# A top-32 attention kernel with routed experts: GpSimd compares the count and multiplies, VectorE only sums, when three thresholds are chosen

## The chip, the cores and the metric

One NeuronCore of a Trainium2 chip runs the whole program. The metric is the device time of one execution in microseconds (us). Engines go by their names in the profile: PE is TensorE, DVE is VectorE, ACT is ScalarE, POOL is GpSimd, SP is SyncE, which only starts DMAs here.

## The reference

Attention for 8 batches of 8 heads, 576 rows of 64 columns, in which each row of scores keeps only its 32 largest; then a layer of 8 experts that routes each of the 4608 tokens to one expert.

```python
scores = scale * np.matmul(q, k.transpose(0, 1, 3, 2))
kth = np.partition(scores, -top_k, axis=-1)[..., -top_k:-top_k + 1]
scores = np.where(scores >= kth, scores, -1000000000.0)
attn = softmax(scores); out = np.matmul(attn, v)
...
logits = x @ w_gate + modality_bias[modality_id]
e_idx = np.argmax(logits, axis=1)
out[mask] = gate_w[mask, None] * (np.maximum(x[mask] @ w1[e], 0.0) @ w2[e])   # for each e
```

## The kernel before, in words

The scores are worked on in 288 tiles of 128 rows by 576 columns; a pair of heads makes nine tiles. The loop `for i in range(LAST)` (line 887) takes one step for each tile, and a step holds one stage of each of the tiles in flight, so that tile i is multiplied while older tiles are further on. The order of the instructions on each engine is the order in which the loop issues them; no scheduler changes it.

What a tile goes through:

- `qk` and `sevac` (lines 323 and 340): the scores, and their copy to SBUF by ScalarE.
- `subs` and `chain` (lines 346 and 351), on VectorE: seven maxima over sevenths of the row (L349) give 56 candidates, and a chain of MAX8 and MATCH_REPLACE8 over these (L360 to L362) gives the 24 largest, `mg[.., 0:24]`.
- `below` (line 370, L374 on GpSimd) sets a bias just below the 24th value; `sign` (L381 on ScalarE) compares the row with it and counts, into `n`, how many values lie below; `pool_y` (L387 on GpSimd) multiplies the row by that comparison, and `find` (L391 on VectorE) takes the next eight values out of the product into `mg[.., 24:32]`.
- `pick` (line 393), once for three tiles: `eq` (L398) compares the count `n` with nine possible counts, `jk` (L399) multiplies the hits by the nine candidates `mg[.., 23:32]`, and a sum (L400) leaves the one threshold of each tile in `kth`. All three are VectorE's, on 128 x 27 numbers.
- `keep` (L411 on VectorE) is the mask: it compares the row with `kth` and multiplies the exponentials `ex` by the result. For two tiles in three of the first 48, `hide` (L418), `hidden` (L424 on GpSimd) and `masked` (L430) do this in another way.
- `trans`, `evac`, `av`: the transposes and the product with v.

Step i handles `chain` of tile i - 1, `pool_y` of tile i - 4, `find` of tile i - 5 and `keep` of tile i - 7 (LY, LT and LR, lines 39 to 41). When (i - 5) % 3 is 2, it also chooses the thresholds of tiles i - 7, i - 6 and i - 5, and the first of these is masked in the same step, right behind. Such a step is called a choosing step below; there are 96.

VectorE's order in a step (lines 1008 to 1047): the chain (`a_`) woven with the maxima and `find` (`b_`), then the list `c_`: `pick`, small work of the routing and of the experts, and `keep` last. Up to four of the seven maxima are held back and put between the last entries of `c_` (HOLD, lines 1040 to 1044), so that an instruction of `pick` does not stand directly behind the one whose result it reads.

GpSimd's order in a step: what `c_` holds for it (the scatter DMAs of finished tokens, `send`, line 562, L564 and the memset L490 behind it; a few copies), then `gate` (L434), `pool_y`, `below`, `small` (L368), `fill` (L314) and at the end the DMAs of expert results (L754). `gate` reads one number of the last tile's mask, so `pool_y` starts only when VectorE has finished the mask of the step before.

The experts' work is issued beside the attention as TensorE has room by a table of costs, and goes on behind it; from about 1060 us on only experts are left.

Of the kernel before, what the change touches and what calls it, by code (L numbers as in the profile page):

```python
# [14 lines left out]
OP = mybir.AluOpType  # L15
AX = mybir.AxisListType
# [22 lines left out]
LY = KL + 2  # L39
LT = LY + 1  # L40
LR = LT + 2
# [30 lines left out]
def kernel(  # L72
# [13 lines left out]
    V, A, G, PE, SP = nc.vector, nc.scalar, nc.gpsimd, nc.tensor, nc.sync  # L86
# [27 lines left out]
    LD, PR, T = {}, {}, {}  # L114
# [43 lines left out]
    def fiota(name, shape, pattern, base, cm):  # L158
        t = const.tile(shape, FT, name=name)
        G.iota(t, pattern=pattern, base=base, channel_multiplier=cm, allow_small_or_imprecise_dtypes=True)  # L160
        return t

    i9s = fiota("i9s", [128, 3, 9], [[0, 3], [2, 9]], S - 2 * TOPK, 0)
# [19 lines left out]
    kth = const.tile([128, NT], FT, name="kth")  # L183
# [200 lines left out]
    def pool_y(i):  # L384
        t = T[i]
        t["y"] = wk.tile([128, S], FT, name="y", bufs=YB)
        G.tensor_tensor(t["y"], t["S"], t["K"], op=OP.mult)  # L387

    def find(i):
        t = T[i]  # L390
        V.max(t["mg"][:, i % 3, 24:32], t["y"])  # L391

    def pick(i):

        t = T[i]
        eq, v = (wk.tile([128, 3, 9], FT, name=nm, bufs=1) for nm in ("eq", "jk"))
        n = t["n"][:, 0, :]
        return [lambda: V.tensor_tensor(eq, i9s, n[:, :, None].to_broadcast([128, 3, 9]), op=OP.is_equal),  # L398
                lambda: V.tensor_tensor(v, eq, t["mg"][:, :, 23:32], op=OP.mult),  # L399
                lambda: V.tensor_reduce(kth[:, i - 2:i + 1], v, axis=AX.X, op=OP.add)]  # L400

    def expo(i):
        t = T[i]
# [28 lines left out]
    def gate(i):  # L432

        G.tensor_scalar(spare[:, 0:1], T[i]["P"][0:1, 0:1], 1.0, 1.0, op0=OP.mult, op1=OP.mult)  # L434
# [247 lines left out]
    def expert(s, act, nxt, whole, defer):  # L682
# [82 lines left out]
        if nxt:  # L765
            pick, rows, done, tok = sched(s + 1, whole)
            todo = pick + done + rows + tok
            c, k = len(todo) - 2, 2 if whole else 3
            cut = [min(k * x, c) for x in range(CUT[0])] + [c + 1] * (CUT[1] - CUT[0]) + [c + 2]

            def both(f, a, b):
                f()
                chore.extend(todo[a:b])
                if not defer:
                    chores()
            n = len(cut) - 1
            return [(c, lambda f=f, a=a, b=b: both(f, a, b), w) for (c, f, w), a, b in zip(main, cut, cut[1:])] + main[n:]
# [13 lines left out]
    def ready(n, whole):  # L791
        pick, rows, done, tok = sched(n, whole)
        for f in pick + done + rows + tok:
            f()
        for g in range(4):
            load_w1(n, g)
        for g in range(4):
            load_w2(n, g)
# [4 lines left out]
    def more_moe():  # L803
# [14 lines left out]
        elif full >= n + 1:  # L818
            now = SL[n - 1] if moe else {"xt": True, "used": [4, 4]}
            if not now["xt"]:  # L820
                return
            plan.update(ready=n, go=False)
            pick, rows, done, tok = sched(n, fits(n))
            free = []

            def begin():
                free.extend(now["used"])
                now["nxt"] = True

            def take(x, g):  # L830
                return lambda: (load_w1, load_w2)[x](n, g) if g < free[x] else None
            l1 = [take(0, g) for g in range(4)]
            l2 = [f for g in range(4) for f in (take(1, g), PAUSE)]
            go = [lambda: plan.update(go=True)]
            if n == 0:
                def sent():

                    while sends:
                        sends.popleft()()
                rush.extend(pick + [begin] + l1[:2] + done + [PAUSE, sent] + rows + [PAUSE, l1[2], l1[3], PAUSE] + tok + go)  # L840
            else:
                rush.extend(pick + [begin] + rows + l1[:1] + done + [PAUSE, l1[1], PAUSE, l1[2], l1[3], PAUSE] + tok + go)
            side.extend(l2)

    def weave(a, b):

        nb, na, kb = len(b), len(a), 0
        for x in range(na):
            a[x]()
            e = (x + 1) * nb // na  # L850
            while kb < e:
                b[kb]()
                kb += 1
        while kb < nb:
            b[kb]()
            kb += 1
# [22 lines left out]
    ok = lambda x: 0 <= x < NT  # L879
    early = lambda u: u < EARLY and u % 3 != 2  # L880
# [6 lines left out]
    for i in range(LAST):  # L887
# [120 lines left out]
        a_, b_, c_ = [], [], []  # L1008
# [4 lines left out]
        if ok(i - LT):  # L1013
            b_.insert(2, lambda: find(i - LT))
            if (i - LT) % 3 == 2:
                c_ += pick(i - LT)
        for x, f in enumerate(lo):
            b_.insert(LOP[x] if x < len(LOP) else len(b_), f)
        small_ = []
# [20 lines left out]
        if ok(i) and len(c_) > 1:  # L1040
            n = min(len(c_) - 1, HOLD)
            held, b_ = b_[len(b_) - n:], b_[:len(b_) - n]
            m = len(c_) - n
            c_ = c_[:m] + [f for pair in zip(held, c_[m:]) for f in pair]
        weave(a_, b_)
        for f in c_:
            f()

        for f in moves:
            f()  # L1050

        if ok(i - 1 - LR) and not early(i - 1 - LR):
            gate(i - 1 - LR)
        if ok(i - LY):
            pool_y(i - LY)
        if ok(i - 1):
            below(i - 1)
        if ok(i - 2) and (i - 2) % 3 == 2:
# [264 lines left out]
```

## Time and profile before

| what | us |
|---|---|
| median of 3 runs | 1294.63 (1292.91 to 1297.9) |
| profiled execution | 1286.85 |
| its span, first to last instruction | 1285.1 |
| VectorE busy in the span | 1157.5 (90%) |
| TensorE busy (matmuls) | 1183.2 (92%) |
| ScalarE busy | 996.6 (78%) |
| GpSimd busy | 665.8 (52%) |

The profiled execution is 7.8 us below the median of the timed runs. Shares are averages over the attention (to about 1060 us) and the experts' tail. A duration in the profile runs from an instruction's start to its end; the next one of the same engine can start before that end, so what an instruction costs its engine is read from start to start.

### The profile page before, as it was taken

What the parts mean: (1) busy time and instruction counts of PE and PEld (TensorE: products, weight loads), DVE (VectorE), ACT (ScalarE), POOL (GpSimd) and SP (SyncE); (2) the same over time, 40 slices, a digit from 0 to 9 for tenths busy, and PEclk for the clock granted to TensorE, in tenths of its full rate; (3) what the DMA queues carried; (4) which work ended last, traced back from release to release, by engine and by line L of the source; (5) the groups of instructions that cost most, each with busy time, mean ns of one, the idle gap of its engine ahead of it and who ended that gap; (6) DMA issues with size and microseconds to landing.
All of it is one profiled execution on the core that took longest, in us unless ns stands there. A gap on an engine that the chain in (4) does not pass through costs nothing. (4 is left out here: it accounts for less than half of the span.)

```text
span 1285.1 us, 29038 instructions
## 1 busy us (share of the span) xinstructions
PE 1183.2 (92%) x8117; PEld 934.1 (73%) x8117; DVE 1157.5 (90%) x5948; ACT 996.6 (78%) x2029; POOL 665.8 (52%) x1249
## 2 busy tenths in 40 slices
PE   5789887999988999999999999999999999999996
PEld 4667676767766778686777868777777766789885
DVE  4999999999999999999999999999999992767752
ACT  3799988888888988888898889888988773446542
POOL 2688866555474557554755575556655562110110
PEclk8899999999999999999999999999999999999998
DMA  6565336765347745755665665656766433657550
GB/s 125 125 183 142 89 85 183 198 156 149 85 128 189 216 124 154 199 158 127 194 169 159 168 187 147 171 143 171 170 154 168 132 122 115 234 186 266 204 171 15
DMA packets 206755, 201.05 MB, mean 156 GB/s; under 512 B 106221, under 2 KB 153325, under 8 KB 206576
## 3 DMA queue, kind: packets, MB, share of 16 engines
q1 hardware_dynamic: 198896, 178.59, 52.6%
q0 software_dynamic: 6256, 19.69, 4.2%
q8 instruction: 69, 1.13, 0.4%
q10 hardware_dynamic: 1424, 0.74, 0.2%
q14 instruction: 110, 0.90, 0.2%
HBM read 118.63 MB, written 24.23 MB: 111 GB/s over the span
## 5 line engine op out<-in xcount | busy, mean ns | idle before, releaser
L349 DVE MAX8 cand<-Ssb 128x8 f32<-128x82 f32 (+1 forms) x2016 | 429.4, 230 | 17.9 <-ACT Ssb L342 17.7
L387 POOL TENSOR_TENSOR y<-Ssb,K 128x576 f32<-128x576 f32 x288 | 367.8, 1277 | 1.9 <-ACT K L381 1.6
L336 PE MATMUL S<-ks,qs 128*128 128x288 f32 x1024 | 230.1, 347 | 43.1 <-ACT Ssb L342 24.5
L342 ACT ACTIVATE Ssb<-S 128x576 f32<-128x576 f32 x288 | 188.7, 655 | 91.4 <-PE S L336 61.7
L381 ACT ACTIVATE K<-Ssb,n 128x576 bf16<-128x576 f32 x288 | 227.5, 790 | 25.3 <-POOL y L387 25.1
L336 PEld LDWEIGHTS S<-ks,qs 128*128 128x128 f32 x1024 | 157.4, 192 | 97.0 <-issue 40.5
L391 DVE MAX8 mg<-y 128x8 f32<-128x576 f32 x288 | 214.4, 745 | 2.7 <-POOL y L387 2.7
L405 ACT ACTIVATE ex<-Ssb,sm 128x576 f32<-128x576 f32 x256 | 200.3, 782 | 0.0
L453 ACT ACTIVATE PT<-T 128x640 f32<-128x640 f32 (+1 forms) x288 | 191.1, 663 | 9.5 <-PE T L445 9.5
L727 PE MATMUL E<-xgT,w1b 128*128 128x256 f32 x768 | 187.6, 387 | 6.8 <-ACT hT L731 3.1
L411 DVE SCALAR_TENSOR_TENSOR P<-Ssb,kth,ex 128x576 f32<-128x576 f32 x224 | 188.6, 842 | 0.3
L739 PE MATMUL E<-w2b,hT 128*128 128x512 f32 x384 | 179.6, 596 | 3.0 <-ACT ot L749 1.7
L445 PE MATMUL T<-idf,P 128*128 128x128 f32 x1152 | 171.9, 277 | 9.5 <-ACT P L430 8.9
L727 PEld LDWEIGHTS E<-xgT,w1b 128*128 128x128 f32 x768 | 139.8, 192 | 31.6 <-ACT hT L731 6.4
L434 POOL TENSOR_SCALAR spare<-P 1x1 f32<-1x1 f32 x224 | 43.6, 195 | 201.7 <-DVE mg L360 186.8
L445 PEld LDWEIGHTS T<-idf,P 128*128 128x128 f32 x1152 | 136.0, 141 | 16.7 <-ACT P L430 13.3
L473 PE MATMUL X<-PT,vm 128*64 128x256 f32 (+1 forms) x1536 | 145.6, 332 | 2.4 <-DVE cand L349 1.1
L374 POOL TENSOR_SCALAR n<-mg 128x1 f32<-128x1 f32 x288 | 72.8, 253 | 133.6 <-DVE mg L362 127.0
L473 PEld LDWEIGHTS X<-PT,vm 128*64 128x64 f32 x1536 | 89.2, 137 | 47.8 <-issue 10.1
L739 PEld LDWEIGHTS E<-w2b,hT 128*128 128x128 f32 x384 | 67.2, 190 | 60.6 <-issue 53.2
L1166 POOL DMA_INDIRECT out_dram<-ot,tk x14 | 14.0, 1003 | 132.3 <-ACT ot L1165 132.3
L862 PE MATMUL E<-idf,onesb 128*128 128x256 bf16 x436 | 63.1, 285 | 0.0
(212 smaller groups left out, 2295.8 us busy)
## 6 DMA issues: line engine op xcount, KB each, us to landing
w1b<-in_moe_w_dram SPq DMA_DIRECT2D x76, 512.0 KB, 5.0
w2b<-in_moe_w_dram SPq DMA_DIRECT2D x76, 512.0 KB, 4.9
qs<-st SPq DMA_DIRECT2D x126, 144.0 KB, 3.5
ks<-st SPq DMA_DIRECT2D x63, 288.0 KB, 3.8
ks<-st SPq DMA_DIRECT2D x62, 256.0 KB, 5.2
xg<-xs SPq DMA_DIRECT2D x19, 516.0 KB, 3.9
km<-in_k_dram SPq DMA_DIRECT2D x64, 128.0 KB, 3.5
vm<-in_v_dram SPq DMA_DIRECT2D x32, 256.0 KB, 3.2
```

What stands on the lines that cost most here:

```text
L336: PE.matmul(ps[:, hf, u - a:v - a], l, d["ks"][:, x, h, u + o:v + o], start=(n == 0), stop=(n == len(terms) - 1), skip_group_check=(j == 8))
L342: A.activation(sb.rearrange("p (a b) -> p a b", a=2), T[i]["ps"][:, :, :288], AF.Copy, scale=0.125)
L349: return [lambda s=s: V.max(c[:, s * 8:s * 8 + 8], T[i]["S"][:, bnd[s]:bnd[s + 1]]) for s in range(NSUB)]
L381: A.activation(t["K"], t["S"], AF.Sign, scale=2.0 ** -24 - 1.0, bias=t["n"][:, 1, i % 3:i % 3 + 1], accum_out=t["n"][:, 0, i % 3:i % 3 + 1])
L387: G.tensor_tensor(t["y"], t["S"], t["K"], op=OP.mult)
L391: V.max(t["mg"][:, i % 3, 24:32], t["y"])
L405: A.activation(t["ex"], t["S"], AF.Exp, bias=t["s"][:, i % 3:i % 3 + 1])
L445: PE.transpose(T[i]["pt"][:, x, :], (Pm if c == 4 else Pb[c % 2])[:, h * 512 + x * 128:h * 512 + x * 128 + 128], idf)
L453: A.activation(o, T[i]["pt"][:, :n], AF.Copy)
L473: PE.matmul(o.rearrange("p (a b) -> p a b", a=2) if j < 8 else o, l, r, start=(c == 0), stop=(c == 4))
L727: PE.matmul(ps[:, f % 2], w1b[:, c, f * 128:(f + 1) * 128], xgT[:, c, :], start=(c == 0), stop=(c == KC - 1))
L739: PE.matmul(o["py"], hT[:, f, t * 128:(t + 1) * 128], w2b[:, f, :], start=(f == 0), stop=(f == FC - 1))
```

## The change

`pick` is split. Its comparison and product go to GpSimd, the comparison as two instructions (a difference, then a test for zero), and VectorE keeps the sum, now called `take`. `gate`, `pool_y` and the new `pick` are issued before the list `c_` of the step, and no longer behind it.

```diff
         n = t["n"][:, 0, :]
-        return [lambda: V.tensor_tensor(eq, i9s, n[:, :, None].to_broadcast([128, 3, 9]), op=OP.is_equal),
-                lambda: V.tensor_tensor(v, eq, t["mg"][:, :, 23:32], op=OP.mult),
-                lambda: V.tensor_reduce(kth[:, i - 2:i + 1], v, axis=AX.X, op=OP.add)]
+        G.tensor_tensor(eq, i9s, n[:, :, None].to_broadcast([128, 3, 9]), op=OP.subtract)
+        G.tensor_scalar(eq, eq, 0.0, 1.0, op0=OP.is_equal, op1=OP.mult)
+        G.tensor_tensor(v, eq, t["mg"][:, :, 23:32], op=OP.mult)
+        t["v"] = v
+
+    def take(i):
+
+        V.tensor_reduce(kth[:, i - 2:i + 1], T[i]["v"], axis=AX.X, op=OP.add)
...
             if (i - LT) % 3 == 2:
-                c_ += pick(i - LT)
+                c_.append(lambda: take(i - LT))
...
         weave(a_, b_)
-        for f in c_:
-            f()
-
-        for f in moves:
-            f()
-
         if ok(i - 1 - LR) and not early(i - 1 - LR):
             gate(i - 1 - LR)
         if ok(i - LY):
             pool_y(i - LY)
+        if ok(i - LT) and (i - LT) % 3 == 2:
+            pick(i - LT)
+        for f in c_:
+            f()
+
+        for f in moves:
+            f()
+
         if ok(i - 1):
             below(i - 1)
```

In the changed kernel's lines the three instructions of GpSimd are L398 to L400, the sum is L405, the mask L416, the gate L439, the send L569 and its memset L495; the experts' small instructions L624 and L645 are L629 and L650.

VectorE in the choosing step that lies at 613 to 617 us, from the end of the chain (L362) to the mask; before:

```order
L362 MAX mg<-cand_10520 128x8
L349 MAX cand<-Ssb 128x8
L398 TENSOR_TENSOR eq<-i9s,n 128x27
L349 MAX cand<-Ssb 128x8
L399 TENSOR_TENSOR jk<-eq,mg 128x27
L349 MAX cand<-Ssb 128x8
L400 TENSOR_REDUCE kth<-jk 128x3
L349 MAX cand<-Ssb 128x8
L411 SCALAR_TENSOR_TENSOR P_123,den_129<-Ssb,kth,ex 128x576
```

and the same piece in the changed kernel:

```order
L349 MAX cand<-Ssb 128x8
L362 MAX mg<-cand_10574 128x8
L349 MAX cand<-Ssb 128x8 x2
L405 TENSOR_REDUCE kth<-jk 128x3
L349 MAX cand<-Ssb 128x8
L416 SCALAR_TENSOR_TENSOR P_123,den_129<-Ssb,kth,ex 128x576
```

Two instructions are gone, one maximum has moved in front of L362, and the sum has as before one maximum between it and the mask.

VectorE in the choosing step at 648 to 651 us, where `c_` also holds the experts' small chain (L624, L645); before:

```order
L362 MAX mg<-cand_11058 128x8
L349 MAX cand<-Ssb 128x8
L624 SCALAR_TENSOR_TENSOR s_jk,s_sc<-s_oh,s_sc,roff 128x8
L398 TENSOR_TENSOR eq<-i9s,n 128x27
L624 SCALAR_TENSOR_TENSOR s_jk,s_sc<-s_oh,ie 128x8
L399 TENSOR_TENSOR jk<-eq,mg 128x27
L645 TENSOR_SCALAR sei_136<-s_sc 1x2
L400 TENSOR_REDUCE kth<-jk 128x3
L349 MAX cand<-Ssb 128x8 x4
L411 SCALAR_TENSOR_TENSOR P_123,den_129<-Ssb,kth,ex 128x576
```

and changed:

```order
L362 MAX mg<-cand_11115 128x8
L349 MAX cand<-Ssb 128x8
L629 SCALAR_TENSOR_TENSOR s_jk,s_sc<-s_oh,s_sc,roff 128x8
L405 TENSOR_REDUCE kth<-jk 128x3
L629 SCALAR_TENSOR_TENSOR s_jk,s_sc<-s_oh,ie 128x8
L650 TENSOR_SCALAR sei_136<-s_sc 1x2
L349 MAX cand<-Ssb 128x8 x4
L416 SCALAR_TENSOR_TENSOR P_123,den_129<-Ssb,kth,ex 128x576
```

The sum now stands where `eq` stood, with the rest of the small chain and four maxima behind it.

GpSimd in the choosing step at 898 to 902 us, which also has a send, with the engines whose semaphores each instruction waits on in brackets (an instruction without brackets waits on none); before:

```order
L314 TENSOR_SCALAR qbd_118<-qs 128x64 [waits DMAHW1_49,DMAHW0_49]
L564 DMA xs<-x_156,dest 38912x516
L490 MEMSET spare 1x1 [waits Pool_49]
L434 TENSOR_SCALAR spare<-P_123 1x1 [waits DVE_49,Pool_49]
L387 TENSOR_TENSOR y<-Ssb,K 128x576 [waits Activation_49]
L374 TENSOR_SCALAR n<-mg 128x1 [waits DVE_49]
L368 TENSOR_SCALAR sm<-mg 128x3
```

and changed:

```order
L439 TENSOR_SCALAR spare<-P_123 1x1 [waits DVE_49,Pool_49]
L387 TENSOR_TENSOR y<-Ssb,K 128x576 [waits Activation_49]
L398 TENSOR_TENSOR eq<-i9s,n 128x27
L399 TENSOR_SCALAR eq<-eq 128x27 [waits Pool_49]
L400 TENSOR_TENSOR jk<-eq,mg 128x27 [waits DVE_49,Pool_49]
L569 DMA xs<-x_156,dest 38912x516
L495 MEMSET spare 1x1
L374 TENSOR_SCALAR n<-mg 128x1 [waits DVE_49]
L368 TENSOR_SCALAR sm<-mg 128x3
```

Gate and product have moved ahead of the send; the three new instructions stand behind the product `y`, and the send, `below` (L374) and `small` (L368) behind them.

## Rows read from the trace of the kernel before

**Rows 1.** The first part of the page: busy time of each engine, its share of the span and its instructions.

```profile
PE 1183.2 (92%) x8117; PEld 934.1 (73%) x8117; DVE 1157.5 (90%) x5948; ACT 996.6 (78%) x2029; POOL 665.8 (52%) x1249
```

**Rows 2.** The view by windows: busy time in microseconds of PE, PEld, DVE, ACT and POOL (instructions in brackets), then the granted clock, the DMA share and GB/s. The first three stretches lie in the attention, the last is the tail after it.

```profile
100.00:160.00 60.00, 53.10 (x444) 41.84 (x443) 60.00 (x335) 56.69 (x129) 50.98 (x68) 1.00 0.47 109
500.00:600.00 100.00, 96.99 (x645) 74.59 (x644) 99.28 (x557) 85.66 (x176) 53.21 (x106) 1.00 0.64 164
900.00:1000.00 100.00, 95.82 (x673) 75.07 (x673) 99.62 (x550) 89.71 (x186) 55.97 (x110) 1.00 0.65 160
1060.00:1285.00 225.00, 203.01 (x1263) 174.78 (x1259) 127.27 (x342) 99.78 (x157) 26.89 (x63) 0.97 0.50 170
```

**Rows 3.** The view of waits, VectorE's own: what it waited for, microseconds in total, times, the longest.

```profile
DVE cand L349 <- ACT Ssb L342: 17.7, 2, 17.0
...
DVE mg L391 <- POOL y L387: 2.7, 6, 0.6
```

**Rows 4.** Groups of VectorE's instructions, shapes kept apart: busy microseconds, mean nanoseconds of one, idle time before them.

```profile
L411 DVE SCALAR_TENSOR_TENSOR P<-Ssb,kth,ex 128x576 f32<-128x576 f32 x224 | 188.6, 842 | 0.3
...
L398 DVE TENSOR_TENSOR eq<-i9s,n 128x27 f32<-128x27 f32 x96 | 20.4, 212 | 0.0
L399 DVE TENSOR_TENSOR jk<-eq,mg 128x27 f32<-128x27 f32 x96 | 19.6, 205 | 0.1
```

**Rows 5.** The same three lines by source line: shortest, median and longest duration in nanoseconds.

```profile
L398 DVE TENSOR_TENSOR eq<-i9s,n x96: 157/169/1330, 37.0 to 1057.6; 128x27 f32<-128x27 f32 x96
L399 DVE TENSOR_TENSOR jk<-eq,mg x96: 157/170/1257, 37.3 to 1057.8; 128x27 f32<-128x27 f32 x96
L411 DVE SCALAR_TENSOR_TENSOR P<-Ssb,kth,ex x224: 787/802/1930, 47.6 to 1059.2; 128x576 f32<-128x576 f32 x112
```

**Rows 6.** VectorE's instructions in order of time in a step that chooses thresholds, 613 to 617 us: start and duration in microseconds.

```profile
613.25 0.08 DVE L411 DVE_READ_ACCUMULATOR Pm<-Ssb,kth,ex 128x1 f32 x1
...
615.23 0.16 DVE L398 TENSOR_TENSOR eq<-i9s,n 128x27 f32<-128x27 f32 x1
615.32 0.23 DVE L349 MAX8 cand<-Ssb 128x8 f32<-128x82 f32 x1
615.47 0.17 DVE L399 TENSOR_TENSOR jk<-eq,mg 128x27 f32<-128x27 f32 x1
615.56 0.23 DVE L349 MAX8 cand<-Ssb 128x8 f32<-128x82 f32 x1
615.72 0.16 DVE L400 TENSOR_REDUCE kth<-jk 128x3 f32<-128x27 f32 x1
...
615.98 0.82 DVE L411 SCALAR_TENSOR_TENSOR P<-Ssb,kth,ex 128x576 f32<-128x576 f32 x1
```

**Rows 7.** GpSimd in the same step: start, duration, and in brackets the idle time before and what ended it.

```profile
613.49 0.18 POOL L434 TENSOR_SCALAR spare<-Pm 1x1 f32<-1x1 f32 x1 [1.36 <-DVE mg L360]
613.63 1.27 POOL L387 TENSOR_TENSOR y<-Ssb,K 128x576 f32<-128x576 f32 x1
615.25 0.20 POOL L374 TENSOR_SCALAR n<-mg 128x1 f32<-128x1 f32 x1 [0.34 <-DVE mg L362]
615.51 0.20 POOL L368 TENSOR_SCALAR sm<-mg 128x3 f32<-128x3 f32 x1
```

**Rows 8.** Both engines in order of time, 897 to 902 us, a step that chooses thresholds and also has a send (L564).

```profile
896.88 1.23 DVE L411 SCALAR_TENSOR_TENSOR P<-Ssb,kth,ex 128x576 f32<-128x576 f32 x1
...
898.05 0.07 DVE L411 DVE_READ_ACCUMULATOR P<-Ssb,kth,ex 128x1 f32 x1
...
898.86 0.99 POOL L564 DMA_INDIRECT xs<-x,dest  x1 [0.16 <-issue]
...
900.16 1.33 DVE L398 TENSOR_TENSOR eq<-i9s,n 128x27 f32<-128x27 f32 x1
900.17 1.27 POOL L387 TENSOR_TENSOR y<-Ssb,K 128x576 f32<-128x576 f32 x1
```

**Rows 9.** The same view at 757 us: a mask and the product y beside it.

```profile
757.72 1.93 DVE L411 SCALAR_TENSOR_TENSOR P<-Ssb,kth,ex 128x576 f32<-128x576 f32 x1
757.76 1.27 POOL L387 TENSOR_TENSOR y<-Ssb,K 128x576 f32<-128x576 f32 x1
```

**Rows 10.** A group of GpSimd's small instructions: busy microseconds, mean nanoseconds of one, idle before them.

```profile
L314 POOL TENSOR_SCALAR qbd<-qs 128x64 fp32r<-128x64 f32 x64 | 20.9, 342 | 2.7 <-DMA ks<-st 0.2
```

**Rows 11.** Two of GpSimd's lines by source line: shortest, median and longest duration in nanoseconds.

```profile
L374 POOL TENSOR_SCALAR n<-mg x288: 189/192/978, 23.6 to 1047.2; 128x1 f32<-128x1 f32 x144
L387 POOL TENSOR_TENSOR y<-Ssb,K x288: 1263/1274/1787, 29.2 to 1055.1; 128x576 f32<-128x576 f32 x144
```

**Rows 12.** GpSimd in order of time at 1018.8 us: the second of the two overwrites what the first reads.

```profile
1018.80 0.21 POOL L590 TENSOR_SCALAR x<-tokb 128x5 f32<-128x5 f32 x1
1019.10 0.20 POOL L591 TENSOR_SCALAR tokb<-tokb 128x5 f32<-128x5 f32 x1
```

**Rows 13.** Both engines at 640 us: a product y and the maximum that waited for it.

```profile
639.29 1.27 POOL L387 TENSOR_TENSOR y<-Ssb,K 128x576 f32<-128x576 f32 x1
...
640.60 0.76 DVE L391 MAX8 mg<-y 128x8 f32<-128x576 f32 x1 [0.58 <-POOL y L387]
```

**Rows 14.** Both engines in order of time at 648 to 650 us, a choosing step with small work of the expert part in it.

```profile
647.87 1.27 POOL L387 TENSOR_TENSOR y<-Ssb,K 128x576 f32<-128x576 f32 x1
...
649.62 0.18 DVE L398 TENSOR_TENSOR eq<-i9s,n 128x27 f32<-128x27 f32 x1
```

More of the change, by code (lines that the diff above doesn't have):

```diff
@@ L1045 @@
         weave(a_, b_)
+        if ok(i - 1 - LR) and not early(i - 1 - LR):
+            gate(i - 1 - LR)
+        if ok(i - LY):
+            pool_y(i - LY)
+        if ok(i - LT) and (i - LT) % 3 == 2:
+            pick(i - LT)
         for f in c_:
@@ L1050 @@
             f()
[L1052 to L1055, printed above, removed]
         if ok(i - 1):
```

## The prediction, on record before the run

> **What bounds the kernel now.** I read the page first. By shares over the whole span TensorE (92%) stands above VectorE (90%) [rows 1], which says little, since attention and tail are mixed. The windows part them [rows 2]. In the attention VectorE is busy for all 60.00 us of one stretch, 99.28 of 100 in another and 99.62 in a third, and in the first of these TensorE has 53.10 us of 60: it is not full, and the steps still come no faster than VectorE allows. After 1060 us VectorE has 127 of 225 us, and nothing of this change runs there. The waits confirm it [rows 3]: VectorE waited 17.0 us for the first scores, and all its waits for the product y sum to 2.7. So in the attention a microsecond taken from VectorE's row of instructions is a microsecond of the program, and one put in as a wait is lost. The reader should next look at how the parts of one choosing step lie in time, on VectorE and on GpSimd [rows 6, 7].
>
> **Removed from VectorE.** Comparison and product took 20.4 + 19.6 = 40 us of busy time [rows 4], but that isn't their price. They overlap their neighbours: the next instruction starts 0.09 us after each (615.23 to 615.32, 615.47 to 615.56 [rows 6]). So 96 x 2 x 0.09 = **17.3 us**.
>
> Beside that some of them were stretched: the means of 212 and 205 ns [rows 4] stand above medians of 169 and 170 [rows 5]. 96 x 43 + 96 x 35 ns = **7.5 us**. One such row shows why: a comparison of 1.33 us lies exactly beside a product y of 1.27 us [rows 8]. Off VectorE, they can't be stretched there.
>
> **Gate, y and pick ahead of the list c_.** In that same step the send (0.99 us) went first on GpSimd, and y began at 900.17, 2.05 us after the mask before it had ended (898.05 + 0.07) [rows 8]; in the plain step it began 0.30 us after (613.33 to 613.63 [rows 6, 7]). With the send behind, y is on time again. A late y also falls on the next mask: 1.93 us beside a y that began 0.04 us later [rows 9], against a median of 0.802 [rows 5]. The masks' mean of 842 against that median is 224 x 40 ns = 9.0 us in all [rows 4, 5]. Some 2 us of it I put to masks of the first 170 us, where another instruction (L424) delays y, and 1 to a late result DMA, both of which stay. I take **6 us** as gone (ends 0 and 9). The send runs later by about 2 us; it is covered, since its tokens are only read by expert slots much later, and n and sm behind it are needed one and two steps on.
>
> **Put on GpSimd, and the new wait.** The sum now waits for GpSimd. What counts is from the end of y to the sum's start. The three instructions on 27 numbers have no row. One number costs 0.192, the 576 of y 1.274 [rows 11], so a two-input one on 27 is about 0.19 + 27 x 1.08/576 = 0.24 and a one-input one 0.21 (64 numbers have a mean of 0.342 with holds [rows 10], an upper end). The first waits for nothing and can start 0.03 before y's end, as y does after the gate (613.63 against 613.67 [rows 7]). The other two wait for the one before: 0.09 from an end to the next start, as between 1018.80 + 0.21 and 1019.10 [rows 12]. From GpSimd to VectorE it is 0.04 (639.29 + 1.27 to 640.60 [rows 13]). Sum: -0.03 + 0.24 + 0.09 + 0.21 + 0.09 + 0.24 + 0.04 = **0.88 us**. Ends: 0.50, with starts 0.15 apart as between gate and y [rows 7], and 1.21, with 0.34 for each.
>
> Against it stands the time VectorE has left. In the plain step y ends at 614.90 [rows 7], and the sum, at 615.72 with the two gone in front of it, is reached at 615.54 [rows 6]: 0.64 us, so it waits 0.24, more than the 0.18 it saved. Where the experts' small chain shares the list, the sum takes the comparison's old place: 649.62 against a y that ends at 649.14 [rows 14], 0.48 us and a wait of 0.40. Worked like this for the 95 choosing steps from 48 to 1050 us, with y on time behind a send: 11 steps have 0.13 on average, 22 have 0.46, 42 have 0.65, and 20 have 1.03. At 0.88 they wait 11 x 0.75 + 22 x 0.42 + 42 x 0.23 + about 0.3 = **27.4 us**. Behind the waiting sum stand a maximum and the mask, with up to four maxima and small instructions between; gate and y of the next step follow the mask. Everything shifts together.
>
> [...] Three numbers that lie apart cost GpSimd 0.20 in the plain step, one number 0.20 [rows 7], so short rows inside an operand cost nothing to see. [...]
>
> **Sum.** -17.3 - 7.5 - 6 + 27.4 = -3.4 us. Against the profiled execution, 1286.85 with 1.75 us around its span, that is 1283.4. That execution is 7.8 us below the median of the runs; the same step from the median gives **1291.2**. About 0.5%, 6.5 us, is what a measurement of this kernel can tell from no change.
>
> **Rivals.**
> 1. *GpSimd is quicker than I add up, and what stays is the stretches that vanish.* With 0.76 us (0.19 for each instruction) the wait is 11 x 0.63 + 22 x 0.30 + 42 x 0.11 = 18.1, the sum -12.7, the time 1281.9; at 0.50 it is 1269. It decides from 0.84 down. For it: VectorE's comparison and product were harmed by y, and copies on GpSimd start 0.15 apart when nothing waits. Against it: two of the three do wait.
> 2. *Slower: the wait at the sum eats more than is saved.* From 0.92 us on it is a loss, from 1.00 on a visible one. At 1.08 the waits are 11 x 0.95 + 22 x 0.62 + 42 x 0.43 + 2 = 44, the time 1308; at 1.21 it is 1321. For it: the margin of the plain step is under 0.88 already, and the 0.342 of a small one [rows 10]. Against it: that mean holds waits.
> 3. *Slower by another way: the mask is held by GpSimd's small instructions.* n and sm now come right behind the product, just when the mask starts. Once 0.20 for each of 96 masks is 19 us: 1310. Against it: in the plain step the comparison (0.16) began 0.02 before n and was not stretched [rows 6, 7]. [...]
> 4. *Nothing comes of it:* TensorE at 97 of 100 us [rows 2] takes over as the bound: 1294.6. Against it: steps are as dense on VectorE where TensorE has 53 of 60.
>
> **How the numbers follow.** My forecast (chain between 0.84 and 1.00) 0.36; rival 1 0.35; rival 2 0.16; rival 3 0.06; rival 4 0.07. So faster 0.35, the same 0.36 + 0.07 = 0.43, slower 0.22. The range reaches from 1277 (a chain of 0.70) to 1306 (1.06) and leaves out about a tenth on each side. The forecast's own range is 1288 to 1301.
>
> **What would show it.** VectorE's busy time falls by 35 to 40 us, but a new wait of the sum for GpSimd's product stands first among its waits in the attention, 0.2 to 0.3 us in most of 96 steps. The three instructions show 0.24, 0.21, 0.24 and start about 0.30 apart. No choosing step has a comparison beside y; masks over 1.1 us are gone; y starts 0.3 us after the mask also in steps with a send. I am wrong if the sum hardly waits (rival 1), if it waits over 35 us (rival 2), or if masks become longer (rival 3).

## The result, and the profile after

The changed kernel takes **1303.43 us** (median of 13 runs, 1298.53 to 1309.98) against 1292.91 (13 runs, 1288.87 to 1297.9) on the same chip. The ratio is **1.0087** [1.0068, 1.0105]: slower by some 11 us. The forecast was 1291.2, no change; it came out as in the second rival, in whose words "the wait at the sum eats more than is saved". The traces differ by more than the medians, 1303.8 against 1285.1 us of span, since the profiled execution of before lies 6 us under its median and that of after 2 above. So sums of trace rows are compared with the traces, and verdicts rest on the timed ratios.

TensorE's granted clock does not explain the loss: from 100 to 1040 us it is 1.00 before, 0.99 after, and 0.99 also in e2 below, which is faster than the kernel before. From the last maximum over y to the end it is 228.2 us before, 230.1 after and 230.3 in e2.

The page's first part, as [rows 1]:

```profile
PE 1193.6 (92%) x8117; PEld 941.7 (72%) x8117; DVE 1129.7 (87%) x5756; ACT 998.4 (77%) x2029; POOL 737.4 (57%) x1537
```

VectorE does 27.8 us less and the program takes longer all the same. VectorE's waits, as [rows 3] (total, times, longest in microseconds):

```profile
DVE kth L405 <- POOL jk L400: 45.6, 82, 2.4
...
DVE cand L349 <- ACT Ssb L342: 18.6, 2, 17.9
```

The sum's wait for GpSimd's product is the longest entry: 45.6 us where the forecast had 27.4. The windows, as [rows 2], show the same thing from the other side:

```profile
500.00:600.00 100.00, 95.85 (x630) 74.77 (x630) 95.66 (x532) 86.01 (x178) 62.67 (x140) 1.00 0.66 172
900.00:1000.00 100.00, 97.22 (x676) 75.19 (x676) 94.68 (x507) 89.16 (x186) 66.37 (x146) 0.98 0.65 170
```

VectorE, full before in both stretches, now idles for 4 to 5 of 100 us. By source line (shortest, median, longest in nanoseconds), as [rows 5]:

```profile
L398 POOL TENSOR_TENSOR eq<-i9s,n x96: 226/227/236, 37.2 to 1074.0; 128x27 f32<-128x27 f32 x96
L399 POOL TENSOR_SCALAR eq<-eq x96: 350/354/422, 37.5 to 1074.4; 128x27 f32<-128x27 f32 x96
...
L416 DVE SCALAR_TENSOR_TENSOR P<-Ssb,kth,ex x224: 786/801/1770, 48.4 to 1076.3; 128x576 f32<-128x576 f32 x112
```

The difference (L398) is as short as estimated. The test for zero (L399) is not: 354 ns at the median and 350 at the shortest, so it is that long also where nothing holds it. The masks' median hasn't moved (802 before).

Both engines in a plain choosing step, as [rows 6, 7] (start, duration, idle time before and what ended it):

```profile
622.62 1.28 POOL L387 TENSOR_TENSOR y<-Ssb,K 128x576 f32<-128x576 f32 x1
...
623.86 0.23 POOL L398 TENSOR_TENSOR eq<-i9s,n 128x27 f32<-128x27 f32 x1
...
624.18 0.36 POOL L399 TENSOR_SCALAR eq<-eq 128x27 f32<-128x27 f32 x1
...
624.62 0.24 POOL L400 TENSOR_TENSOR jk<-eq,mg 128x27 f32<-128x27 f32 x1
...
624.90 0.18 DVE L405 TENSOR_REDUCE kth<-jk 128x3 f32<-128x27 f32 x1 [0.24 <-POOL jk L400]
624.95 0.19 POOL L374 TENSOR_SCALAR n<-mg 128x1 f32<-128x1 f32 x1
624.99 0.24 DVE L349 MAX8 cand<-Ssb 128x8 f32<-128x83 f32 x1
...
625.18 0.82 DVE L416 SCALAR_TENSOR_TENSOR P<-Ssb,kth,ex 128x576 f32<-128x576 f32 x1
```

From y's end (623.90) to the sum it is 1.00 us, and it is 0.98 to 1.00 in most steps in which the sum waits (median 0.99): test and product start 0.32 and 0.44 after the one before. GpSimd's n (624.95, 0.19) is over before the mask starts.

The other kind of step, at 775 to 781 us:

```profile
774.65 1.03 POOL L569 DMA_INDIRECT xs<-x,dest  x1 [0.17 <-issue]
...
775.60 0.09 DVE L416 DVE_READ_ACCUMULATOR P<-Ssb,kth,ex 128x1 f32 x1
...
775.86 0.19 POOL L374 TENSOR_SCALAR n<-mg 128x1 f32<-128x1 f32 x1
...
776.13 0.45 POOL L314 TENSOR_SCALAR qbd<-qs 128x64 fp32r<-128x64 f32 x2
...
776.75 1.05 POOL L759 DMA_INDIRECT out_dram<-ot,stok  x1 [0.16 <-issue]
...
777.98 0.18 POOL L439 TENSOR_SCALAR spare<-P 1x1 f32<-1x1 f32 x1
...
778.13 1.27 POOL L387 TENSOR_TENSOR y<-Ssb,K 128x576 f32<-128x576 f32 x1
...
780.40 0.18 DVE L405 TENSOR_REDUCE kth<-jk 128x3 f32<-128x27 f32 x1 [2.44 <-POOL jk L400]
```

The mask ended at 775.69. The send of the step before had gone behind its y, as the change wants, and pushed n, the filling and a result DMA behind that mask; so y of this choosing step begins 2.44 us after the mask, where it was 0.24 in the plain step (622.38 to 622.62), and the sum waits 2.44 us instead of 0.24. Sorted by what stands ahead of y, 10 such steps with a DMA wait **15.7 us**, 6 with a filling alone 3.6, and the other 79 from 40 us on 26.3, 0.33 each.

An issue itself takes GpSimd about 1 us, 0.9 to 1.6; the sends by source line (shortest, median, longest in nanoseconds):

```profile
L569 POOL DMA_INDIRECT xs<-x,dest x40: 905/1059/1635, 202.5 to 1105.4; - x40
```

The masks' group, as [rows 4]:

```profile
L416 DVE SCALAR_TENSOR_TENSOR P<-Ssb,kth,ex 128x576 f32<-128x576 f32 x224 | 184.2, 822 | 0.2
```

**The sum again, with measured sizes:** -17.3 (two instructions) - 7.5 (their stretches) - 4.9 (masks: mean 842 [rows 4] to 822, so 224 x 20 ns = 4.5, and 0.4 of the 32 middle ones) + 45.6 = +15.9 us. From the first to the last maximum over y (L391) the attention takes 1026.3 us before and 1042.2 after: +15.9. That the two agree to the tenth is chance: there is one trace of each kernel, and the medians of the timed runs differ by 10.5 us where the spans of the traces differ by 18.7.

### The profile page after: what moved, and what is told of

Its sections match the earlier page's. It is cut to its first block, busy times and chain, and to the rows that moved or that the text cites. A ratio compares the mean times of both kernels' runs of the same rounds, so it can differ in the third digit from the quotient of the medians.

```text
span 1303.8 us, 29134 instructions
## 1 busy us (share of the span) xinstructions
PE 1193.6 (92%) x8117; PEld 941.7 (72%) x8117; DVE 1129.7 (87%) x5756; ACT 998.4 (77%) x2029; POOL 737.4 (57%) x1537
## 5 line engine op out<-in xcount | busy, mean ns | idle before, releaser
L349 DVE MAX8 cand<-Ssb 128x8 f32<-128x82 f32 (+1 forms) x2016 | 421.8, 229 | 18.8 <-ACT Ssb L342 18.6
L391 DVE MAX8 mg<-y 128x8 f32<-128x576 f32 x288 | 213.9, 743 | 0.0
L416 DVE SCALAR_TENSOR_TENSOR P<-Ssb,kth,ex 128x576 f32<-128x576 f32 x224 | 184.2, 822 | 0.2
L478 PE MATMUL X<-PT,vm 128*64 128x256 f32 (+1 forms) x1536 | 148.6, 336 | 2.1 <-DVE cand L349 0.8
L439 POOL TENSOR_SCALAR spare<-P 1x1 f32<-1x1 f32 x224 | 40.4, 181 | 170.3 <-DVE mg L360 105.4
L374 POOL TENSOR_SCALAR n<-mg 128x1 f32<-128x1 f32 x288 | 66.1, 229 | 107.4 <-DVE mg L362 92.5
```

What stands on the lines that cost most here:

```text
L349: return [lambda s=s: V.max(c[:, s * 8:s * 8 + 8], T[i]["S"][:, bnd[s]:bnd[s + 1]]) for s in range(NSUB)]
L478: PE.matmul(o.rearrange("p (a b) -> p a b", a=2) if j < 8 else o, l, r, start=(c == 0), stop=(c == 4))
```

## Experiments

"Ratio" is always to the kernel before. "Attention" is the time from the first to the last of the 288 maxima over y in the profiled execution.

| kernel | ratio [95%] | sum's wait, us | attention, us |
|---|---|---|---|
| before | 1 | none | 1026.3 |
| changed | 1.0087 [1.0068, 1.0105] | 45.6 | 1042.2 |
| e1: difference and test early | 0.9954 [0.9939, 0.9969] | 20.9 | 1023.1 |
| e2: the order alone | 0.9936 [0.9913, 0.9959] | none | 1019.0 |
| e3: sends first | 1.0223 [1.0201, 1.0245] | - | - |
| e4: one product more | 1.0309 [1.0291, 1.0327] | 72.9 | 1066.8 |
| e5: shorter test | 1.0025 [1.0013, 1.0038] | 33.3 | 1032.9 |
| e6b: the order, no choice | 0.9904 [0.9889, 0.9919] | none | 1015.0 |
| e7: DMAs held back | 1.0141 [1.0124, 1.0157] | 35.7 | 1044.5 |
| e8: e1, DMAs held back | 0.9973 [0.9956, 0.9989] | 9.9 | 1025.0 |
| e10: comparison alone moved | 0.9942 [0.9924, 0.9960] | 3.1 (product) | 1019.8 |
| e11: e2, fewer experts beside | 1.0025 [1.0011, 1.0038] | none | 1015.9 |
| e12: e6b, fewer experts beside | 0.9957 [0.9937, 0.9977] | none | 1007.0 |
| e13: sends ahead of the other y | 1.0134 [1.0101, 1.0167] | 40.4 | 1046.0 |

**e2, the order alone.** The kernel before, with its three instructions on VectorE:

```diff
+        if ok(i - 1 - LR) and not early(i - 1 - LR):
+            gate(i - 1 - LR)
+        if ok(i - LY):
+            pool_y(i - LY)
         for f in c_:
             f()
...
-        if ok(i - 1 - LR) and not early(i - 1 - LR):
-            gate(i - 1 - LR)
-        if ok(i - LY):
-            pool_y(i - LY)
```

> Edit: the kernel before with only gate and y issued ahead of the list c_; the choosing stays on VectorE. Theory A: no sum waits for GpSimd, so the order alone gains what stretches vanish, about 7 us of 13 since some y stay late behind pushed DMAs: ratio 0.995 (0.991 to 0.999). Theory B: the order is the loss, ratio 1.004 or more. [...]

Hit: 8 us faster, and the interval lies below theory B's 1.004. VectorE is busy 6.1 us less (1151.4), 4.8 of it in the group of masks (183.8). The order is a gain by itself, so moving the choice to GpSimd, which the change did on top of it, cost 1.5%, some 20 us.

**e5, a shorter test.** Square of the difference, subtraction and a maximum in place of test, product and sum:

```diff
-        G.tensor_scalar(eq, eq, 0.0, 1.0, op0=OP.is_equal, op1=OP.mult)
-        G.tensor_tensor(v, eq, t["mg"][:, :, 23:32], op=OP.mult)
+        G.tensor_tensor(eq, eq, eq, op=OP.mult)
+        G.tensor_tensor(v, t["mg"][:, :, 23:32], eq, op=OP.subtract)
...
-        V.tensor_reduce(kth[:, i - 2:i + 1], T[i]["v"], axis=AX.X, op=OP.add)
+        V.tensor_reduce(kth[:, i - 2:i + 1], T[i]["v"], axis=AX.X, op=OP.max)
```

> Edit: in place of the zero test (0.354 us) the square of the difference, and the candidates minus the square in place of the product; VectorE takes the largest instead of the sum. Same number of instructions on each engine. Theory A: the chain falls by the shorter middle instruction, 0.12 us (0.24 for 0.354), in some 82 waiting steps: waits 45.6 to about 36 us, ratio 1.001 (0.998 to 1.004). [...]

```profile
L399 POOL TENSOR_TENSOR eq<-eq x96: 231/232/311, 37.7 to 1065.2; 128x27 f32<-128x27 f32 x96
```

Hit. The middle instruction falls from 354 to 232 ns, the chain from 1.00 to 0.86 us, almost the forecast's 0.88; the wait falls by 12.3 us and the time by 0.6%, some 8 us. So the test's length cost about that, and with the forecast's chain the change still isn't a gain.

**e4, one product more**, the hits times 1, between test and product:

```diff
+        G.tensor_scalar(eq, eq, 1.0, 1.0, op0=OP.mult, op1=OP.mult)
```

> The changed kernel with one more small product on GpSimd (the hits times 1) between the test and the product, so that the chain from the end of y to the sum is longer by about 0.21 + 0.09 = 0.30 us. Theory A (what GpSimd's chain takes beyond VectorE's margin is lost one for one): some 88 of the 96 sums already wait, so 88 x 0.29 = 25 us more than the changed kernel, ratio to the kernel before 1.028 (1.024 to 1.032); the sum's wait grows from 45.6 to about 71 us. Rival B (the steps have slack elsewhere, on TensorE or in what is issued for the experts, and a wait at the sum is partly made good later): under 1.020.

```profile
L399 POOL TENSOR_SCALAR eq<-eq x96: 350/352/428, 37.5 to 1098.9; 128x27 f32<-128x27 f32 x96
L400 POOL TENSOR_SCALAR eq<-eq x96: 227/228/235, 37.9 to 1099.4; 128x27 f32<-128x27 f32 x96
```

Hit. Wait +27.3 us, attention +24.6, time +2.2% (some 28 us): the chain is lost one for one. The two rows are the control on the test's price: the same tile, one input each, 352 ns with the test for zero in it and 228 with products alone.

**e1, difference and test early**, ahead of gate and y, and only the product (`pick_v`) behind:

```diff
+        if ok(i - LT) and (i - LT) % 3 == 2:
+            pick(i - LT)
         if ok(i - 1 - LR) and not early(i - 1 - LR):
             gate(i - 1 - LR)
         if ok(i - LY):
             pool_y(i - LY)
         if ok(i - LT) and (i - LT) % 3 == 2:
-            pick(i - LT)
+            pick_v(i - LT)
```

> Edit: difference and zero test are issued ahead of the gate, only the product stays behind y. Theory A (all the loss is VectorE waiting at its sum, for a chain of 0.99 us behind y): the chain behind y shrinks to about 0.25 us, the waits at the sum fall from 45.6 us to about 10, what is left being the steps with a late y; with 29.6 us saved on VectorE the time is 20 us below the kernel before, ratio 0.985 (0.980 to 0.990). Theory B (the loss is the DMAs that the new order pushes into the next step): no gain on the changed kernel, ratio 1.006 to 1.011. [...]

Faster than the changed kernel by 1.3%, but against the kernel before it gains 0.5% where 1.5% were expected. The wait stayed at 20.9 us, 15.0 of it in 11 steps with a DMA ahead:

```profile
763.02 1.05 POOL L763 DMA_INDIRECT out_dram<-ot,stok  x1 [0.16 <-issue]
...
764.13 0.25 POOL L398 TENSOR_TENSOR eq<-i9s,n 128x27 f32<-128x27 f32 x1
764.47 0.37 POOL L399 TENSOR_SCALAR eq<-eq 128x27 f32<-128x27 f32 x1
764.81 0.18 POOL L443 TENSOR_SCALAR spare<-P 1x1 f32<-1x1 f32 x1
764.96 1.27 POOL L387 TENSOR_TENSOR y<-Ssb,K 128x576 f32<-128x576 f32 x1
766.20 0.23 POOL L405 TENSOR_TENSOR jk<-eq,mg 128x27 f32<-128x27 f32 x1
```

Behind a DMA the two early instructions only push y further, and the sum (766.46) waits 2.26 us.

**e3, sends first.** In the changed kernel sends went ahead of gate and y. The first send of a batch then also passed the copy of its token numbers, so that the experts' data differ; its time isn't comparable, and nothing follows from it.

> Edit: the changed kernel with the scatter DMAs (sends) again ahead of gate and y, as before the change; the three instructions stay behind y. Theory A: the chain stays at 0.99 us, the long waits move from steps behind a send to steps with one, and the masks' stretches come back: ratio 1.007 to 1.014. Theory B: the loss goes away, ratio 0.998 to 1.002. [...]

**e7 and e8, DMAs held back** in the step ahead of a choosing one, and the filling one step later, in the changed kernel (e7) and in e1 (e8); sends carry the mark `dma`:

```diff
-            f = side.popleft() if side and not rush else PAUSE
+            f = side.popleft() if side and not rush and not (hasattr(side[0], "dma") and i % 3 == 0) else PAUSE
...
-        if j == 3 and p < NPAIR:
+        if j == 4 and p < NPAIR:
...
-        if sends and seen[0]:
+        if sends and seen[0] and i % 3:
...
-        while puts and puts[0][0] <= 0:
+        while puts and puts[0][0] <= 0 and i % 3:
```

> The changed kernel, but the send and the result DMA are held back by one step when the next step is one that chooses, and the filling of the block-diagonal operand comes one step later, so that gate and y of a choosing step have nothing late ahead of them. In the changed kernel 10 choosing steps with a DMA ahead wait 15.7 us and 6 with a filling 3.6, the other 79 wait 26.3 (0.33 each). Theory A: the 16 wait 0.33 each too, 45.6 goes to about 31.6, and the time falls by 14 us: ratio to the kernel before 0.998 (0.995 to 1.001). Rival B (the held DMAs only make y late in another step, where the maximum that reads it waits instead): 1.005 or above.

> The same holding back of DMAs and the filling in the version that puts difference and test ahead of gate and only the product behind y. There the sum still waits 20.9 us, 15.0 of it in 11 steps with a DMA ahead and 2.9 in 5 early ones with a filling. Theory A: about 4.5 of the 20.9 stay, 16 us less: ratio to the kernel before 0.9954 - 0.0127 = 0.983 (0.979 to 0.986). Rival B (as above, or TensorE as the bound): 0.990 or above.

Theory A fell in both. The sum's wait did fall, by 9.9 and 11.0 us, but e7 is slower than the changed kernel by 0.5%, and e8 no faster than e1. In e7 VectorE is busy 8.0 us longer (1137.7), 5.6 of it in masks; one kind of mask shows why:

```profile
L416 DVE SCALAR_TENSOR_TENSOR Pm<-Ssb,kth,ex x32: 786/800/1949, 67.3 to 1079.7; 128x576 f32<-128x576 f32 x32
```

The longest was 945 ns in the changed kernel. A send behind the choice makes the y of the next step late, and that y runs beside a mask. So rival B holds by its figure and only in part by its mechanism: the maxima over y wait 3.2 us. The experts start a little later as well (8141 matmuls instead of 8117), which clouds the comparison; e13 has not that fault.

**e13**, the changed kernel with the list ahead of gate and y in the steps directly before a choosing one, so that no send changes its step:

```diff
+        if i % 3 == 0:
+            for f in c_:
+                f()
         if ok(i - 1 - LR) and not early(i - 1 - LR):
             gate(i - 1 - LR)
...
-        for f in c_:
-            f()
+        if i % 3:
+            for f in c_:
+                f()
```

> The changed kernel, but in the steps directly ahead of a choosing step the list with the sends goes ahead of gate and y again, as in the kernel before, and the filling comes one step later, behind the product of the choice. No send moves to another step. The y that a send now delays is not the one a sum waits for in the same step. Theory A (the late y of a choosing step is a cost of its own: 10 steps with a DMA ahead wait 15.7 us and 6 with a filling 3.6, against 0.33 in a plain step): the sum's wait goes from 45.6 to about 35, against which some 3 us of stretched masks come back; ratio to the kernel before 1.003 (1.000 to 1.006). Rival B (GpSimd is as late whatever the order, since the same work stands between two masks): waits above 42 us and 1.007 or above.

Rival B, if not by its figure for the wait: that fell by 5.2 us only, VectorE is busy 9.3 us longer (1139.0), and the time is above the changed kernel's. The masks' group (busy microseconds, mean nanoseconds of one, idle time before them):

```profile
L416 DVE SCALAR_TENSOR_TENSOR P<-Ssb,kth,ex 128x576 f32<-128x576 f32 x224 | 190.2, 850 | 0.1
```

The masks are back at the 842 of before [rows 4]. So the 15.7 us of waits behind DMAs are real but no order tried here saves them: an issue holds GpSimd 0.9 to 1.6 us, and that falls on a sum, or on the mask beside the late y.

**e6b, the order and no choice**: e2 with one instruction of the sum's size instead of three, the floor for any placing elsewhere.

```diff
-        return [lambda: V.tensor_tensor(eq, i9s, n[:, :, None].to_broadcast([128, 3, 9]), op=OP.is_equal),
-                lambda: V.tensor_tensor(v, eq, t["mg"][:, :, 23:32], op=OP.mult),
-                lambda: V.tensor_reduce(kth[:, i - 2:i + 1], v, axis=AX.X, op=OP.add)]
+        return [lambda: V.tensor_reduce(kth[:, i - 2:i + 1], t["mg"][:, :, 31:32].to_broadcast([128, 3, 9]), axis=AX.X, op=OP.max)]
```

> The kernel before with gate and y ahead of the list of the step, and with comparison and product left out altogether: the sum is replaced by a maximum over the 32nd value of each tile, of the same size, so the choice by the count is left out and masks may differ in a few values. It prices the two instructions on VectorE by themselves, and is the floor of any placing of them elsewhere. Theory A: they cost 96 x 2 x 0.09 = 17.3 us on top of the order's gain, so ratio 0.9936 - 0.0134 = 0.980 (0.977 to 0.983). A2: they cost about 26 us, which is what the difference of the changed kernel from the order alone (19.6 us) and its waits of 45.6 us leave: 0.973 (0.970 to 0.977). Rival B (TensorE becomes the bound as soon as VectorE has less): 0.986 or above.

Rival B by its figure. Without the two instructions and without any sum that waits for GpSimd the kernel gains 0.3% on e2 (the intervals just overlap), 4 us and not 17. VectorE's waits from 540 to 1050 us say where a part of the rest went:

```profile
DVE x L505 <- PE X L504: 10.0, 6, 3.0
DVE lt L533 <- PE X L525: 3.1, 3, 1.5
```

In e2 these two are 1.6 and 0.7. They are TensorE's transposes for the routing, which stand in its order behind the experts' matmuls. TensorE is busy for 487 of the 500 us from 540 to 1040; in e2, where VectorE hardly waits for it, it is 489, so that busy time alone does not show which engine sets the pace. Another part went to the masks, which take 6.4 us more than in e2 (183.8):

```profile
L409 DVE SCALAR_TENSOR_TENSOR P<-Ssb,kth,ex 128x576 f32<-128x576 f32 x224 | 190.2, 850 | 0.9 <-ACT ex L403 0.8
```

20 masks take over 1 us here, 5 in e2, as where a late y meets a mask [rows 9].

**e11 and e12** are e2 and e6b with less of the experts' work beside the attention:

```diff
-STEP = 3.39
+STEP = 3.28
```

> The kernel before with gate and y ahead of the list, and with less of the experts' work issued beside the attention: the planner may add 3.28 instead of 3.39 us of TensorE's time in a step, so that about 288 x 0.11 = 32 us of it comes behind the attention. It is the control of the next one; the figure to compare is when the last maximum over y starts (1050.9 us in the same order with 3.39). Theory A (VectorE bounds here): that time moves by under 4 us; the whole time grows by 10 to 35 us (ratio 1.00 to 1.02). Rival B (TensorE bounds already here): it comes over 8 us earlier.

> The same smaller share of experts' work, with comparison and product left out (the sum is replaced by a maximum over the 32nd values, as in the version without the choice). With the full share the last maximum over y comes only 3.2 us earlier than with the two instructions, and all of that before 540 us, while VectorE waits 13 us for routing products of TensorE behind it. Theory A (behind 540 us TensorE had become the bound, and ate what VectorE saved): with TensorE relieved the last maximum over y comes 13 to 19 us earlier than in the control, and VectorE's waits for TensorE's products in 540 to 1040 us fall from 13 to under 5 us. Rival B (the two instructions cost VectorE only some 3 us, since they filled gaps): 2 to 6 us earlier.

VectorE's waits in e12 from 540 to 1040 us:

```profile
DVE x L505 <- PE X L504: 6.0, 5, 2.4
DVE cand L349 <- ACT Ssb L342: 0.9, 2, 0.7
DVE lt L533 <- PE X L525: 0.4, 1, 0.4
```

e11's attention ends 2.1 us earlier than e2's, as theory A says: VectorE sets the pace there. e12 lies between the two theories: with TensorE relieved, leaving the two instructions out ends the attention 10.1 us earlier (1038.7 against 1048.8) instead of 3.2; by the table's measure it is 8.9 instead of 4.0, and 8.9 us between the medians of the timed runs. TensorE as the next bound is thus shown for a part of what e6b lost. Of the rest, the waits above are 4.4 us more than e11's 2.0, and the masks take 4.5 us more (189.9 against 185.4); what remains is open.

**e10, the comparison alone**: e1 with product and sum on VectorE.

```diff
-        G.tensor_tensor(t["v"], t["eq"], t["mg"][:, :, 23:32], op=OP.mult)
+        V.tensor_tensor(t["v"], t["eq"], t["mg"][:, :, 23:32], op=OP.mult)
...
-                c_.append(lambda: take(i - LT))
+                c_ += [lambda: pick_v(i - LT), lambda: take(i - LT)]
...
-        if ok(i - LT) and (i - LT) % 3 == 2:
-            pick_v(i - LT)
```

> Only the comparison goes to GpSimd: difference and test ahead of gate and y, while product and sum stay VectorE's, in the order of gate and y of the changed kernel. Nothing waits for a chain behind y any more. Theory A (the order is worth 8 us, an instruction of 0.09 us off VectorE 96 x 0.09 = 8.6 us, of which only the half before some 540 us comes through because TensorE bounds behind that): ratio to the kernel before 0.9936 - 0.0035 = 0.990 (0.988 to 0.993), no wait at product or sum. Rival B (difference and test make gate and y late by 0.3 to 0.6 us in a choosing step, and that costs what the instruction saves): 0.995 or above.

It missed A's range by a little, isn't to be told from e2, and its interval excludes neither theory. The product waits 3.1 us, and the masks take 190.6 us against 183.8 in e2, which is rival B's mechanism: a later y costs about what the instruction saves. Of the versions that choose, e2 and e10 are the quickest, and the floor e6b leaves only 0.3% under them.

## Why the prediction was wrong

The measured 1303.43 lies inside the outer range of 1277 to 1306 and above the forecast's own 1288 to 1301; the sign was wrong.

- **The bound** was right in one half: VectorE's order sets the steps, and a wait put into it is lost (e4: 27.3 us more of wait, 24.6 of attention). The other half, that a microsecond taken from VectorE is a microsecond of the program, did not hold in e6b: the two instructions, 17.3 us from start to start, were worth 4.0 us of attention there.
- **-17.3 and -7.5 for the two instructions, -6 for the masks**: right in the changed kernel. The attention's +15.9 us less the wait of 45.6 leaves -29.7, against -30.8 forecast. But the first term counts in full only here, where the sum's waits make the steps long. On top of the order alone, without those waits, it is worth 4 us (e6b).
- **+27.4 for the wait is the step that failed**, in two places.
- *The chain, 0.88 us.* The forecast's "one-input one 0.21" put the price of a product on a test for zero, which takes 0.354. Difference 0.227, product 0.238, first start -0.04 and release 0.03 came within 0.02. Over some 82 waiting steps the missing 0.11 us are 9 us; e5, with a chain of 0.86, gave 8 of them back.
- *"With the send behind, y is on time again."* True in the send's own step (at 902.38 y began 0.30 us after the mask); the sentence "The send runs later by about 2 us; it is covered" looked at who reads the tokens, and not at what stands behind the send on GpSimd. That was n, a filling, perhaps a result DMA, and then gate and y of the next step. The 10 steps wait 15.7 us where 0.33 each would be 3.3: +12.4. The 6 steps with a filling add 1.6 in the same way. Chain and lateness make 23.0; the difference of 45.6 and 27.4 is 18.2. The 4.8 us too much may lie in the margins read from the trace; no run shows it.
- **Rival 2** named the mechanism and the sign, and its 35 us of wait were passed. Its threshold for a loss, a chain of 0.92, was too kind, since it had no late y in it: e5 loses a little at 0.86.
- **Rival 1** fell with the test; the estimate for the other two instructions was already close.
- **Rival 3** is refuted. A median over all 224 masks (801 against 802) could not show it, as only 80 of them stand right behind a choice; but of these 80 none is longer than 821 ns, and their mean is 809 against 828 before. Where VectorE's instruction was the long one, its recorded start lies ahead of that of y, by 0.01 us for the comparison at 900.16 [rows 8] and by 0.04 for the mask at 757.72 [rows 9]. So which of two will be the long one can't be read from starts that lie this close. The other way about shows as well. In e1 small GpSimd instructions come at a mask, and some of them are long: the difference at 654.14 takes 0.92 us, beside a mask of 0.79 from 654.16. The longest of its difference and test are 926 and 1020 ns:

```profile
L398 POOL TENSOR_TENSOR eq<-i9s,n x96: 227/238/926, 35.3 to 1053.3; 128x27 f32<-128x27 f32 x96
L399 POOL TENSOR_SCALAR eq<-eq x96: 350/356/1020, 35.6 to 1054.1; 128x27 f32<-128x27 f32 x96
```

- **Rival 4** did not decide the changed kernel but is a part of what caps any better placing (leaving the two instructions out is worth 4.0 us in e6b, and 8.9 in e12, where TensorE is relieved).
- **Rows inside an operand.** The two instructions that read one operand in three rows of nine take 227 and 238 ns; on the dense tile alone a two-input product takes 232 (e5) and a one-input one 228 (e4). So rows that lie apart cost nothing to see here, as the prediction had it, and the long instruction, the test with its 354 ns, is one on a dense tile.
- **What would show it.** VectorE's busy time fell by 27.8, not 35 to 40: busy time counts overlapped stretches once, and the next instruction starts 0.09 us after each of the two, which are 0.16 and 0.17 long [rows 6], so the 40 us of two overlapping lines were never all in it. Three masks over 1.1 us are left (1.77, 1.68, 1.60; 12 of this group before), the first two beside a y that a result DMA had made late (370.66, 905.71).

## What to carry to other kernels

Work moved to a less busy engine is priced by its latency from the last input to the reader, not by the idle share of that engine: GpSimd was busy for 665.8 of 1285.1 us before [rows 1], and 0.14 us less in a chain of 1 us gave back some 8 of the 11 us lost (e5). When an instruction is moved past a DMA issue, follow what then stands behind that issue into the next step, up to the next wait that someone is held by: here 10 steps behind a DMA wait 15.7 us. Before work is taken off the bounding engine, look how far the next one is below it, and what the shorter steps will make late: of 17.3 us taken from VectorE e6b kept 4.0. The part of this change that was a gain by itself was the order (e2, 8 us).

## What the runs showed that was not expected

A one-input GpSimd instruction with a test for zero and a product takes 352 to 354 ns on 128 x 27 numbers, the same with two products 228. The delay that GpSimd's DMA issues cause (0.9 to 1.6 us each) was not removed by any order tried: taken off the sums (45.6 to 35.7 and 40.4 us) it came back as 8.0 and 9.3 us of longer VectorE work, masks above all.
